# Bulk token attention and the last gradient stage hand-pipelined by groups of four heads, with the output projection as a stage of its own

## The chip, the cores and the metric

One core of one Trainium2 chip. The metric is device time in microseconds (us) of one execution; a median stands for three or more executions. The kernel computes one forward pass and all gradients of a model with two attention branches.

## The reference, cut to what matters

```python
def _B_ref(x, mem0, Wq, Wk, Wv, Wo, seg_len):      # x: 1 x 2048 x 576, 32 heads of 128, 8 memory rows, segments of 32
    mask = (idx[:, None] < M) | (idx[:, None] >= idx[None, :])
    mem = mem0
    for s in range(n_seg):                          # 64 segments, one after the other
        h = jnp.concatenate([mem, xs], axis=1)
        q, k, v = (einsum('btd,dhe->bhte', h, W) for W in (Wq, Wk, Wv))
        p = _softmax(where(mask, einsum('bhqe,bhke->bhqk', q, k) * scale, -1e9))
        o = einsum('bhte,hed->btd', einsum('bhqk,bhke->bhqe', p, v), Wo)
        mem = o[:, :M, :]                           # the memory rows go on to the next segment
        outs.append(o[:, M:, :])
    return jnp.concatenate(outs, axis=1)
g = _sigmoid((x * gate_w).sum(-1, keepdims=True))
return g * _A_ref(x, ...) + (1 - g) * _B_ref(x, ...)   # and jax.vjp of all that
```

The memory rows form a chain over the segments, which the kernel runs first. Token rows only read the finished memory, so their attention is done afterwards in bulk: 16 tiles of 128 tokens, each in 8 groups of four heads, 128 groups in all.

## The kernel before

Bulk attention, forward and backward, of one group, and the projection at the end of a tile (loads, masks and repeated lines cut):

```python
def b_bulk(self, keep, wp, sp, psum):
    for tt in range(NTT):
        ...                                          # kmT, vmT, block-diagonal k and v of the memory: 10 transfers
        for g in range(8):
            for w in ("q", "k", "v"):                # eight loads of 128 KB, on sync and GpSimd in turn
                self.dq_eng().dma_start(xT[w][:], self.xTd[w][tt][:, 4 * g:4 * g + 4, :])
                self.dq_eng().dma_start(tok[w][:], self.xtok[w][trows, gc])
            ...                                      # dO, dOT
            ...                                      # scores -> Sp; Et = exp (ScalarE); l, r (VectorE)
            nc.gpsimd.tensor_tensor(out=Pn[:], in0=Et[:], in1=r[:]..., op=ALU.mult)
            nc.sync.dma_start(self.px_dram[tt][:, 4 * g:4 * g + 4, :], Pn[:, :, 0:128])
            PT = transp(Pn, "x_PT")
            ...                                      # o = PT v -> o_g, stored; transposed into oTa (kept on chip)
            nc.gpsimd.tensor_tensor(out=prod[:], in0=dOT[:], in1=oT_g, op=ALU.mult)
            ...                                      # dP -> dS, stored; DT; dq, stored; memory rows -> dm_g
            for i, h in enumerate(hs):               # eight stores of 8 KB
                nc.sync.dma_start(self.mtok["dkx"][...], dm_g[r32, 0:128])
                nc.sync.dma_start(self.mtok["dvx"][...], dm_g[r32, 128:256])
        pb = psum.tile([P, 1024], F32, name="x_big", bufs=2)
        self.row_mm(pb, [(oTa[:, h, :], self.WoN[:, h, :]) for h in range(HB)])   # the tile's output projection
        ...                                          # output, gate gradient
```

The last gradient stage:

```python
def b_post(self, keep, sp, psum):
    mB, sB = ...                                     # one block-diagonal buffer each for q, dO, p, ds
    for tt in range(self.NTT):
        for w in ("q", "dO"):
            self.load_blockdiag(mB[w], self.mtok[w], tt)          # 2 x 4 transfers
        for i in range(4):
            for sl in range(4):
                for w, src in (("p", self.pmq_dram), ("ds", self.dsmq_dram)):
                    nc.sync.dma_start(sB[w][...], src[4 * tt + sl]...)   # 32 transfers
        for g in range(8):
            ...                                      # five loads, on sync and GpSimd in turn
            ...                                      # dk, dv, stored; three transposes; 24 products into pdx
```

The softmax here doesn't subtract the row's maximum and nothing guards it: scores larger than these inputs give would overflow.

Of the kernel before, what the change touches and what calls it, by code (L numbers as in the profile page):

```python
# [7 lines left out]
ALU = mybir.AluOpType  # L8
# [22 lines left out]
class Kern:  # L31
# [50 lines left out]
    def setup_B_dram(self, dram):  # L82
# [11 lines left out]
        self.mtok = {w: t(w + "m_dram", [NM, J]) for w in ("q", "k", "v", "o", "dO", "dq", "dk", "dv", "dkx", "dvx")}  # L94
# [8 lines left out]
        self.dsmq_dram = t("dsmq_dram", [NSEG, MEM, HB, 32])  # L103
        self.memT_dram = t("memT_dram", [P, NKT, NSEG, MEM])
# [281 lines left out]
    def b_bulk(self, keep, wp, sp, psum):  # L386
# [13 lines left out]
        self.maskX = mx  # L400
        vmB = [wp.tile([P, 8, 4, E], BF16, name=f"x_vmB{i}") for i in range(2)]
        kmB = [wp.tile([P, 8, 4, E], BF16, name=f"x_kmB{i}") for i in range(2)]
        for t in vmB + kmB:
            nc.gpsimd.memset(t[:], 0.0)
        dgacc = keep.tile([P, D], F32, name="dgacc")
        nc.vector.memset(dgacc[:], 0.0)
        for tt in range(NTT):
            trows = slice(tt * P, (tt + 1) * P)
            mT = {}
            for w in ("k", "v"):  # L410
                mT[w] = sp.tile([P, 4, HB, 8], BF16, name=f"x_{w}mT", bufs=2)
                nc.sync.dma_start(mT[w][:], self.mTd[w][4 * tt:4 * tt + 4].rearrange("s p h t -> p s h t"))
            vB, kB = vmB[tt % 2], kmB[tt % 2]
            self.load_blockdiag(vB, self.mtok["v"], tt)
            self.load_blockdiag(kB, self.mtok["k"], tt)
            xt = sp.tile([P, D], BF16, name="x_xt", bufs=2)
            nc.sync.dma_start(xt[:], self.A_x[trows, :])
            go = sp.tile([P, D], BF16, name="x_go", bufs=2)
            nc.sync.dma_start(go[:], self.grad_out[trows, :])
            at = sp.tile([P, D], BF16, name="x_at", bufs=2)  # L420
            nc.sync.dma_start(at[:], self.a_dram[trows, :])
            oTa = sp.tile([P, HB, P], BF16, name="x_oTa", bufs=1)
            for g in range(8):
                hs = range(4 * g, 4 * g + 4)
                gc = slice(512 * g, 512 * g + 512)
                xT, tok = {}, {}
                for w in ("q", "k", "v"):
                    xT[w] = sp.tile([P, 4, P], BF16, name=f"x_{w}T", bufs=3)
                    self.dq_eng().dma_start(xT[w][:], self.xTd[w][tt][:, 4 * g:4 * g + 4, :])
                    tok[w] = sp.tile([P, 512], BF16, name=f"x_{w}", bufs=3)  # L430
                    self.dq_eng().dma_start(tok[w][:], self.xtok[w][trows, gc])
                dO_g = sp.tile([P, 512], BF16, name="x_dO", bufs=3)
                self.dq_eng().dma_start(dO_g[:], self.xtok["dO"][trows, gc])
                dOT = sp.tile([P, 512], BF16, name="x_dOT", bufs=3)
                self.dq_eng().dma_start(dOT[:], self.xTd["dO"][tt][:, 4 * g:4 * g + 4, :].rearrange("p h t -> p (h t)"))
                Sp = psum.tile([P, 4, 256], F32, name="x_big", bufs=2)
                for b in range(2):
                    self.mm(Sp[:, 2 * b:2 * b + 2, 0:160], lhsT=self.identB[:], rhs=self.maskX[:], start=True, stop=False)
                for i, h in enumerate(hs):
                    q_h = xT["q"][:, i, :]  # L440
                    self.mm(Sp[:, i, 0:128], lhsT=q_h, rhs=xT["k"][:, i, :], start=False, stop=False)
                    self.mm(Sp[:, i, 128:160], lhsT=q_h, rhs=mT["k"][:, :, h, :], start=False, stop=True)
                Et = sp.tile([P, 4, 160], BF16, name="x_E", bufs=2)
                nc.scalar.activation(Et[:], Sp[:, :, 0:160], ACT.Exp, scale=SCALEB)
                l = sp.tile([P, 4], F32, name="x_l", bufs=2)
                nc.vector.tensor_reduce(out=l[:], in_=Et[:], axis=AX.X, op=ALU.add)
                r = sp.tile([P, 4], F32, name="x_r", bufs=2)
                nc.vector.reciprocal(r[:], l[:])
                Pn = sp.tile([P, 4, 160], BF16, name="x_P", bufs=3)
                nc.gpsimd.tensor_tensor(out=Pn[:], in0=Et[:], in1=r[:].unsqueeze(2).to_broadcast([P, 4, 160]), op=ALU.mult)  # L450
                nc.sync.dma_start(self.px_dram[tt][:, 4 * g:4 * g + 4, :], Pn[:, :, 0:128])

                def transp(src, nm):
                    pt = psum.tile([P, 640], BF16, name="x_tr", bufs=2)
                    for i in range(4):
                        self.tr(pt[:, 128 * i:128 * i + 128], src[:, i, 0:128], P)
                    for i in range(4):
                        self.tr(pt[32 * i:32 * i + 32, 512:640], src[:, i, 128:160], P, tp=(0, 32 * i))
                    o = sp.tile([P, 640], BF16, name=nm, bufs=2)
                    nc.vector.tensor_copy(o[:], pt[:])  # L460
                    return o

                def transp4(src, dst):
                    pt = psum.tile([P, 640], BF16, name="x_tr", bufs=2)
                    for i in range(4):
                        self.tr(pt[:, 128 * i:128 * i + 128], src[:, 128 * i:128 * i + 128], P)
                    nc.vector.tensor_copy(dst, pt[:, 0:512])

                PT = transp(Pn, "x_PT")
                po = psum.tile([P, 512], F32, name="x_po", bufs=2)  # L470
                self.mm(po[:], lhsT=PT[:, 512:640], rhs=vB[:, g].rearrange("p i e -> p (i e)"), start=True, stop=False)
                for i, h in enumerate(hs):
                    self.mm(po[:, 128 * i:128 * i + 128], lhsT=PT[:, 128 * i:128 * i + 128],
                            rhs=tok["v"][:, 128 * i:128 * i + 128], start=False, stop=True)
                o_g = sp.tile([P, 512], BF16, name="x_o", bufs=3)
                nc.scalar.copy(o_g[:], po[:])
                nc.sync.dma_start(self.xtok["o"][trows, gc], o_g[:])
                oT_g = oTa[:, 4 * g:4 * g + 4, :].rearrange("p h t -> p (h t)")
                transp4(o_g, oT_g)
                prod = sp.tile([P, 512], BF16, name="x_prod", bufs=2)  # L480
                nc.gpsimd.tensor_tensor(out=prod[:], in0=dOT[:], in1=oT_g, op=ALU.mult)
                dP = psum.tile([P, 4, 256], F32, name="x_big", bufs=2)
                for i, h in enumerate(hs):
                    hc = slice(128 * i, 128 * i + 128)
                    self.mm(dP[:, i, 0:128], lhsT=dOT[:, hc], rhs=xT["v"][:, i, :], start=(i % 2 == 0), stop=False)
                    self.mm(dP[:, i, 128:160], lhsT=dOT[:, hc], rhs=mT["v"][:, :, h, :], start=False, stop=False)
                    self.mm(dP[:, i, 0:160], lhsT=prod[:, hc], rhs=self.negones[:], start=False, stop=True)
                dS = sp.tile([P, 4, 160], BF16, name="x_dS", bufs=3)
                nc.vector.scalar_tensor_tensor(out=dS[:], in0=dP[:, :, 0:160], scalar=SCALEB, in1=Pn[:],
                                               op0=ALU.mult, op1=ALU.mult)  # L490
                nc.sync.dma_start(self.dsx_dram[tt][:, 4 * g:4 * g + 4, :], dS[:, :, 0:128])
                DT = transp(dS, "x_DT")
                pq = psum.tile([P, 512], F32, name="x_po", bufs=2)
                self.mm(pq[:], lhsT=DT[:, 512:640], rhs=kB[:, g].rearrange("p i e -> p (i e)"), start=True, stop=False)
                for i, h in enumerate(hs):
                    self.mm(pq[:, 128 * i:128 * i + 128], lhsT=DT[:, 128 * i:128 * i + 128],
                            rhs=tok["k"][:, 128 * i:128 * i + 128], start=False, stop=True)
                dq_g = sp.tile([P, 512], BF16, name="x_dq", bufs=3)
                nc.scalar.copy(dq_g[:], pq[:])  # L499
                nc.sync.dma_start(self.xtok["dq"][trows, gc], dq_g[:])  # L500
                pk = psum.tile([P, 512], F32, name="x_po", bufs=2)
                for i, h in enumerate(hs):
                    r32 = slice(32 * i, 32 * i + 32)
                    self.mm(pk[r32, 0:128], lhsT=dS[:, i, 128:160], rhs=tok["q"][:, 128 * i:128 * i + 128], tp=(0, 32 * i))
                    self.mm(pk[r32, 128:256], lhsT=Pn[:, i, 128:160], rhs=dO_g[:, 128 * i:128 * i + 128], tp=(0, 32 * i))
# [937 lines left out]
```

## Time and profile before

| what | before |
|---|---|
| median | 9572.9 us (9568.9 to 9580.3, 4 runs) |
| bulk with projection, 3720 to 5400 | 1680 us, 13.1 us a group |
| backward chain beside the other branch, 5400 to 7562 | 2162 us |
| last gradient stage, 7562 to 8602 | 1040 us |
| granted TensorE clock in bulk, in the last stage | 0.63, 0.81 |

A stage is read from a window of the trace: busy time of each engine, the granted clock, and the mean share in which the 16 DMA engines were busy. The prediction shows the windows and waits of bulk. One line more, the largest wait of TensorE in the last stage (who waited, for whom; us in total, times, longest):

```profile
PE y_pk L66 <- DMA y_dsB<-dsmq_dram: 364.1, 15, 24.7
```

### The profile page before, as it was taken

To read this page: it belongs to the slowest core of one execution; us is meant where nothing else is said; L and a number is where in the kernel's file an instruction comes from. 1 tells how busy PE (TensorE), PEld (TensorE's weight loads), DVE (VectorE), ACT (ScalarE), POOL (GpSimd) and SP (SyncE) were. 2 spreads that over 40 slices of the span, in tenths; PEclk is the share of its full clock that TensorE was granted. 3 is DMA by queue.
4 is the path that set the end of the run, shared out by engine and by line. 5 is a ranking of instruction groups with operands and counts; after the bars stand their busy time and mean duration, and the time that the engine had idled before them with its cause. 6 is when DMAs were issued, how large, how long until landed. Compare 5 with 4: busy or idle time off the path is not lost. (4 is left out here: it accounts for less than half of the span.)

```text
span 9566.9 us, 226296 instructions
## 1 busy us (share of the span) xinstructions
PE 7831.6 (82%) x91018; PEld 3772.5 (39%) x91416; DVE 4114.3 (43%) x7885; ACT 3642.1 (38%) x6854; POOL 1360.6 (14%) x2452
## 2 busy tenths in 40 slices
PE   7899899999999995555555499999999856565997
PEld 2444444444444442333333244444444333333444
DVE  4222266666666662222222277777777511111001
ACT  2333355555555552111111166666666411111000
POOL 2000000011001103333333200000000111111002
PEclk9999788888888886666666688888888688788998
DMA  3554422222222223555555533333333344446443
GB/s 110 208 198 180 169 35 37 35 36 36 37 35 36 37 34 103 144 140 142 144 141 144 162 75 74 75 74 74 76 74 75 91 118 133 116 131 240 148 149 129
DMA packets 1667936, 1002.79 MB, mean 105 GB/s; under 512 B 1103017, under 2 KB 1568498, under 8 KB 1644546
## 3 DMA queue, kind: packets, MB, share of 16 engines
q1 hardware_dynamic: 1596354, 733.66, 29.8%
q0 software_dynamic: 70528, 254.63, 8.1%
q8 instruction: 716, 11.73, 0.5%
q14 instruction: 338, 2.77, 0.1%
HBM read 597.23 MB, written 390.53 MB: 103 GB/s over the span
## 5 line engine op out<-in xcount | busy, mean ns | idle before, releaser
L1052 DVE TENSOR_TENSOR a_W<-a_dP,a_E 128x512 bf16<-128x512 f32 x2048 | 1328.3, 686 | 797.3 <-PE a_dP L66 757.3
L1185 DVE TENSOR_TENSOR b_dS<-b_dP,b_E 128x512 bf16<-128x512 f32 x2048 | 1313.6, 684 | 611.9 <-PE b_dP L66 509.1
L1018 ACT ACTIVATE a_E<-a_S 128x512 bf16<-128x512 f32 x2048 | 1137.9, 598 | 649.7 <-PE a_dP L66 550.2
L1164 ACT ACTIVATE b_E<-b_S 128x512 bf16<-128x512 f32 x2048 | 1110.0, 595 | 505.0 <-PE b_dP L66 307.8
L66 PE MATMUL b_dP<-b_KV,b_QD 32*128 32x512 bf16 x2048 | 663.9, 444 | 21.3 <-DVE b_dS L1185 20.9
L66 PE MATMUL b_S<-b_KV,b_QD 32*128 32x512 bf16 x2048 | 550.4, 446 | 116.0 <-DMA b_QD<-qd_dram 92.8
L66 PE MATMUL a_dP<-a_QD,l_KV 32*128 32x512 bf16 x2048 | 590.9, 424 | 49.9 <-DVE a_W L1052 49.9
L66 PE MATMUL a_S<-a_QD,l_KV 32*128 32x512 bf16 x2048 | 560.7, 424 | 8.7 <-DMA a_QD<-qd_dram 8.0
L66 PE MATMUL w_acc<-w_d,w_h 128*128 128x512 bf16 (+1 forms) x2352 | 522.5, 380 | 38.5 <-DMA w_d<-dqx_dram 35.8
L731 DVE COPY y_T<-y_pt 128x512 bf16<-128x512 bf16 x384 | 151.2, 422 | 888.3 <-PE y_pt L71 888.3
L66 PE MATMUL r_pj<-WT,r_dT 128*32 128x288 bf16 x12288 | 497.7, 309 | 0.0
L63 ACT CAST p_tok<-p_pb 128x512 bf16<-128x512 f32 x512 | 299.5, 586 | 514.1 <-PE p_pb L66 514.1
L66 PE MATMUL b_acc<-b_dS,b_SD 128*32 128x512 bf16 x2048 | 475.3, 460 | 0.0
L66 PE MATMUL b_acc<-b_E,b_SD 128*32 128x512 bf16 x2048 | 474.9, 460 | 0.0
L61 DVE COPY p_tT<-p_pt 128x512 bf16<-128x512 bf16 x512 | 217.5, 425 | 597.0 <-PE p_pt L71 596.8
L66 PE MATMUL a_acc<-a_E,l_VK 128*64 128x512 bf16 x2048 | 443.4, 429 | 24.3 <-DVE a_acs L1060 24.3
L66 PE MATMUL a_acc<-a_W,l_WK 128*64 128x512 bf16 x2048 | 462.5, 448 | 0.0
L66 PE MATMUL y_pdx<-WT,y_T 128*128 128x512 bf16 (+1 forms) x2977 | 422.3, 287 | 23.1 <-ACT y_dx L737 10.9
L499 ACT CAST x_dq<-x_po 128x512 bf16<-128x512 f32 x128 | 75.0, 586 | 939.2 <-PE x_po L66 879.2
L66 PEld LDWEIGHTS <-r_dT 128*32 128x32 bf16 x12288 | 350.8, 105 | 114.5 <-issue 19.9
L66 PEld LDWEIGHTS <-WoN 128*128 128x128 bf16 (+1 forms) x10080 | 338.4, 110 | 100.0 <-issue 100.0
L66 PEld LDWEIGHTS <-w_h 128*128 128x128 bf16 (+1 forms) x2400 | 237.2, 100 | 323.5 <-issue 57.9
(408 smaller groups left out, 12300.3 us busy)
## 6 DMA issues: line engine op xcount, KB each, us to landing
b_QD<-qd_dram SPq DMA_DIRECT2D x256, 128.0 KB
b_SD<-sd_dram SPq DMA_DIRECT2D x256, 128.0 KB
dOx_dram<-p_tok SPq DMA_DIRECT2D x16, 1024.0 KB
dOxT_dram<-p_tT POOLq DMA_DIRECT2D x16, 1024.0 KB, 5.5
kx_dram<-p_tok SPq DMA_DIRECT2D x16, 1024.0 KB
kxT_dram<-p_tT POOLq DMA_DIRECT2D x16, 1024.0 KB, 5.3
vx_dram<-p_tok SPq DMA_DIRECT2D x16, 1024.0 KB
vxT_dram<-p_tT POOLq DMA_DIRECT2D x16, 1024.0 KB, 5.4
```

The costliest lines, as they stand in the source:

```text
L61: nc.vector.tensor_copy(out, in_)
L63: nc.scalar.copy(out, in_)
L66: return self.nc.tensor.matmul(out, lhsT, rhs, start=start, stop=stop, tile_position=tp, skip_group_check=True)
L499: nc.scalar.copy(dq_g[:], pq[:])
L731: nc.vector.tensor_copy(tT[:], pt[:])
L1018: nc.scalar.activation(E_[m][:], S.pop(m)[:, :], ACT.Exp, scale=SCALEA)
L1052: nc.vector.tensor_tensor(out=W_[m][:], in0=dP[:], in1=E_[m][:], op=ALU.mult)
L1164: nc.scalar.activation(E_[m][:], S.pop(m)[:, :], ACT.Exp, scale=SCALEA)
L1185: nc.vector.tensor_tensor(out=D_[m][:], in0=dP[:], in1=E_[m][:], op=ALU.mult)
```

## The change

The intent: break the chain of engines within a group. Seven groups are in flight in bulk and three in the last stage, in hand order (`manual_schedule`: the instructions stay in the order in which the program writes them), each stage of a group one round later than the stage before it. Loads go out three groups ahead, all on the sync queue. The projection leaves bulk (its accumulator's place goes to the pipeline) and reads the transposed o back from DRAM. The four pieces of dm (what the memory rows get of the gradients of k and v) are stored as four transfers of 16 KB instead of eight of 8 KB. The last stage gets two sets of block-diagonal buffers.

```diff
-            for g in range(8):
-                ... one group from loads to dm, as above
+        def load(t):
+            ...
+            for w, nb in (("k", 4), ("q", 4), ("v", 8), ("dO", 8)):
+                d[w + "T"] = sp.tile([P, 4, P], BF16, name=f"x_{w}T", bufs=nb)
+                nc.sync.dma_start(d[w + "T"][:], self.xTd[w][tt][:, 4 * g:4 * g + 4, :])
+            for w, nb in (("v", 6), ("k", 10), ("q", 10), ("dO", 10)):
+                d[w] = sp.tile([P, 512], BF16, name=f"x_{w}", bufs=nb)
+                nc.sync.dma_start(d[w][:], self.xtok[w][tt * P:(tt + 1) * P, 512 * g:512 * g + 512])
+        def st_OT(t):
+            ...
+            nc.scalar.copy(oT[:], pt[:, 0:512])
+            nc.sync.dma_start(self.oxT_dram[tt][:, 4 * g:4 * g + 4, :], oT[:]...)
+        def st_Q(t):
+            ...
+            for i in range(4):
+                nc.sync.dma_start(self.dmx_dram[tt * 32:(tt + 1) * 32, :, h * E:(h + 1) * E], dm[32 * i:32 * i + 32])
+        stages = (st_S, st_T, st_O, st_OT, st_D, st_DT, st_Q)
+        with self.tc.manual_schedule():
+            for t in range(3):
+                load(t)
+            for t in range(NG + len(stages) - 1):
+                for n, st in enumerate(stages):
+                    if 0 <= t - n < NG:
+                        st(t - n)
+                load(t + 3)
+    def b_out(self, wp, sp, psum):
+        for tt in range(self.NTT):
+            nc.sync.dma_start(oTa[:], self.oxT_dram[tt])
+            ...
+            self.row_mm(pb, [(oTa[:, h, :], self.WoN[:, h, :]) for h in range(HB)])
+            ...                                      # ScalarE copy, four VectorE steps -> dz16
+            self.mm(pg[0:1, 0:512], lhsT=dz16[:, 0:1], rhs=xt[:, 0:512])     # the gate row
     def b_post(self, keep, sp, psum):
-        mB = {w: keep.tile([P, 8, 4, E], BF16, name=f"y_{w}B") for w in ("q", "dO")}
+        mB = {w: [keep.tile([P, 8, 4, E], BF16, name=f"y_{w}B{i}") for i in range(2)] for w in ("q", "dO")}
+            if g == 4 and tt + 1 < self.NTT:
+                load_tile(tt + 1)                    # the 40 transfers, on sync
+        stages = (st_KV, st_T, st_H)
```

## The prediction

> **What bounds the kernel now.** I read the page first (its slices and its list of groups), then cut the span into stages with the busy-time windows, then read the waits, the single-tile views and the timeline in the two stages that the change rewrites. The windows are:
>
> ```profile
> core 0: us, PE busy (x) PEld busy (x) DVE busy (x) ACT busy (x) POOL busy (x), PEclk, DMA share, GB/s
> ...
> 3720.00:5400.00 1680.00, 952.55 (x8624) 578.52 (x8735) 462.72 (x895) 282.43 (x528) 588.13 (x773) 0.63 0.52 139
> ...
> 7562.00:8602.00 1040.00, 638.10 (x5776) 373.94 (x5887) 151.23 (x384) 160.14 (x273) 166.72 (x314) 0.81 0.43 124
> ```
>
> The first row is the bulk attention with the output projection inside it: 1680 us for 128 groups of four heads, 13.1 us a group. No engine is above 57%. The second row is the last gradient stage: 1040 us for 128 groups. Everything outside these rows (6847 us) runs the same instructions after the change, so I carry it over unchanged.
>
> In bulk the waits of TensorE show a chain, not a full engine:
>
> ```profile
> PE x_big L66 <- POOL x_prod L481: 255.3, 128, 4.8
> PE x_po L66 <- DMA x_v<-vx_dram: 152.7, 32, 6.8
> PE x_tr L71 <- DVE x_dS L489: 101.1, 108, 1.3
> PE x_tr L71 <- POOL x_P L450: 59.2, 17, 7.3
> ```
>
> A group is scores, exp, sum, reciprocal, normalise, transpose, o, transpose o, product, dP, dS, transpose, dq. Each step waits for another engine, and at most two groups overlap. GpSimd makes P and prod and issues half the loads too. The granted clock is only 0.63.
>
> In the last stage the picture is different. Two windows of one tile (eight groups):
>
> ```profile
> 7567.00:7601.00 34.00, 32.84 (x319) 19.52 (x324) 8.27 (x21) 8.20 (x14) 9.05 (x17) 1.00 0.64 192
> 7601.00:7634.00 33.00, 7.64 (x51) 4.11 (x51) 1.18 (x3) 1.81 (x3) 1.60 (x3) 0.59 0.22 53
> ```
>
> Inside a tile TensorE is full at clock 1.00. The starts of the first matmul of each group lie 4.86 us apart, again and again. Between tiles TensorE stands still: the waits give `y_pk` behind the transfer `y_dsB` 364.1 us in 15 waits, 24.3 us each. Those are single buffers, refilled by 40 transfers after the last reader of the old tile.
>
> Third, the sync queue (SPq), which the busy shares leave out. The single-tile views give the issue time of one transfer (ns, min/median/max):
>
> ```profile
> L431 SPq DMA_DIRECT2D x_k<-kx_dram x128: 320/434/1535, 3619.6 to 5357.9; - x128
> L510 SPq DMA_DIRECT2D dkxm_dram<-x_dm x512: 302/419/1782, 3745.1 to 5391.5; - x171
> L383 SPq DMA_DIRECT2D x_kmB<-km_dram x64: 539/607/610, 3728.6 to 5293.5; - x64
> L702 SPq DMA_DIRECT2D y_pB<-pmq_dram x256: 651/651/719, 7480.7 to 8557.9; - x128
> ```
>
> Adding the durations of all its records in bulk gives 1012 us of 1680, although GpSimd issues 512 loads beside it. After the change it issues all of them. That is the number on which this prediction turns.
>
> **What the Trainium skill says.** (1) "TensorE: Matmul & The Clock Gate", Part 1, the HAM clock gate: an idle window drops the array to half clock and sustained work restores it. The trace agrees: 1.00 inside a tile, 0.59 in the window with the stall, 0.63 in bulk. (2) "Perfetto Trace Analysis", "What DMA-bound means": one way to be DMA-bound is that the issuing engine's sequencer is solid DMA slices. In bulk it is 60% full now, so not yet. (3) "DMA: Bandwidth & Descriptors", "Issuing engines are not separate DMA queues": issuing from several engines only saves the sequencer's time, which is "usually small relative to the DMA itself". Here the trace differs: a 128 KB load costs 0.43 us to issue, and 128 packets of 1 KB at a mean of 56 ns over 16 engines are 0.45 us of engine time. The two are equal, so taking GpSimd out of the issuing is not free.
>
> **The change, part by part: bulk.** Instructions per group stay almost the same, but the program order staggers seven groups, so each engine finds its input made one round earlier. The chain between engines is gone. What remains is the work of each resource in a round:
> - ScalarE: exp 0.70, o 0.59, o transposed (moved here from VectorE) about 0.59, dq 0.59, dm 0.38: 2.85 us.
> - VectorE: 0.82 + 0.18 + 2 x 0.49 + 0.82 = 2.8 us. GpSimd: 1.25 + 1.15 = 2.4 us, its four issues of 0.55 gone.
> - TensorE: from the stretches in the timeline (masks and scores 1.4, transposes 0.8 twice, o 1.0, o transposed 0.4, dP 1.1, dq 1.0, memory rows 0.4) about 7 us at the clock of now; a full clock would give some 4.5.
> - DMA engines: 11 transfers of 1 KB packets x 0.45, two (P, dS) of 512 packets of 256 B at 17.8 ns = 0.57 each, the small ones about 0.8: 6.9 us.
> - Sync queue: the order of the built kernel shows 17 transfers a round (8 loads, 5 stores of 128 KB, 4 of dm) and 10 more per tile. Successive starts are about 0.046 us further apart than the duration. 8 loads x 0.475 = 3.8; P and the four other stores 0.5 + 4 x 0.43 = 2.2; dm 4 x 0.465 = 1.9 (half as many as before, twice the bytes); per tile 8 x 0.65 + 2 x 0.5 = 6.2, over 8 groups 0.8. Sum 8.7 us.
>
> A check from the other side: 1012 us plus some 2150 gaps of 0.046 is 1111; 640 more loads and stores add about 300, 512 fewer dm stores take 248 off, the loads that move to the projection 35: 1128, or 8.8 a group. I add 0.1 for waits on landings. The largest of the five sets the round: the queue, 8.9 us x 128 = 1140, and 25 for filling and draining: **1165 us**.
>
> **Output projection.** 16 tiles, each 32 products of 512 columns (0.216 us) and 32 of 64 (about 0.06) and the gate row: 8.7 us, 139 in all. Its loads hide (three buffers). A start and tail behind the barrier add 13: **152 us**. Together 1317 against 1680: 363 saved.
>
> **Last stage.** TensorE stays at 4.86 a group, 38.9 a tile. The tile's 40 transfers (8 x 0.63 + 32 x 0.695 = 27.3 us of issuing) now go into second buffers four groups ahead, but on the same in-order queue, ahead of the loads of the group three ahead. Until those land it takes 27.3 + 1.9 + 2.5 = 31.7 us. TensorE then has in hand the rest of one round (3.9) and three whole ones (14.6): 18.5. It therefore still stands for 13 us a tile in place of 24, and restarts at the low clock (about 2). A tile: 38.9 + 13 + 2 = 54; the queue's own sum, 8 x 3.1 + 27.3 = 52, agrees. 15 x 54 + 39 + 8 = **857 us**, 183 saved.
>
> Total: 9575 - 363 - 183 = 9029; I say **9030 us**.
>
> **The rivals.** (A) TensorE bounds bulk, not the queue: seven groups in flight leave it no gaps, and 7 us a round give 896 (4.5 with a full clock gives less). For it: it has the next largest sum. Against it: 8.7 of issuing is counted from measured durations. It would make about 8,770. (B) Landings bound it. The trace's records show that each sync-queue transfer signals one of eight semaphores in turn and first waits for the earlier one on it, so eight are in flight. From issue to the last arrival I find medians of 2.0 to 4.3 us. If all 18.25 took 4.3, the round would be 18.25 x 4.3 / 8 = 9.8 us, and the total about 9,145. With DMA engines busy 6.9 of 8.9 this is the likelier miss. (C) The new order buys nothing in bulk: stores that wait for compute stand ahead of the loads on one queue, and the groups end up in lockstep at 12 us; then only the last stage gains: about 9,430. Against it: loads go out three rounds ahead, and buffers (4 to 10) cover seven stages. (D) The last stage's burst is hidden wholly: 16 x 39 + 10 = 634, total 8,805. Against it: the queue needs 52 us a tile whatever TensorE does.
>
> **Range and chances.** Issuing at 0.40 to 0.52 us a transfer, or landings as in (B), moves bulk by -120 to +130; the tile stall (8 to 16 us) moves the last stage by 70. Together: 8,890 to 9,210 eight times in ten. Slower than 9,384 (no 2% gain) needs (C). Faster 0.94, same 0.05, slower 0.01.
>
> **What would show it.** In the changed profile bulk should take about 1165 us with the sync queue over 90% filled, TensorE's longest waits on loads (the transposed q and k) instead of on GpSimd's prod, and a clock under 1. The projection should be near 150 us with TensorE full. The last stage should keep 4.86 us a group, with 15 gaps of 11 to 15 us, behind a load that the burst delays. Wrong would be: a sync queue with long idle stretches in bulk (then A or C), its issues no longer but waits on its own landings (B), no gaps between tiles (D), or a change in the other 6847 us.

## The result, and the profile after

The kernel after took 9428.0 us (median; 9426.3 to 9435.9, 4 runs) beside 9572.9 before: a ratio of 0.985 (95% interval 0.983 to 0.987). That is 1.5% faster, where 9030 (5.7%) was predicted. A ratio here is the mean time of one kernel's runs over that of the other's of the same rounds, so not quite the ratio of the medians. Effects of experiments below are differences of such ratios from 0.985, times 9575 us, except where a run edits the kernel before; the stage times are read from the traces.

The windows of the kernel after, bulk, projection and last stage (busy us and instruction count of each engine, then clock, DMA share, GB/s):

```profile
core 0: us, PE busy (x) PEld busy (x) DVE busy (x) ACT busy (x) POOL busy (x), PEclk, DMA share, GB/s
3722.00:5141.00 1419.00, 746.92 (x7680) 532.43 (x7679) 333.16 (x641) 336.66 (x640) 318.95 (x265) 0.65 0.67 172
5141.00:5370.00 229.00, 158.15 (x1056) 73.17 (x1056) 53.52 (x128) 10.22 (x16) 7.07 (x15) 0.86 0.46 148
7501.00:8461.00 960.00, 634.60 (x5891) 390.35 (x5888) 152.62 (x384) 147.65 (x273) 0.00 (x0) 0.84 0.51 136
```

| part | before | after | saved | predicted |
|---|---|---|---|---|
| bulk, projection | 1680 | 1419 + 229 = 1648 | 32 | 363 |
| backward chain | 2162 | 2131 | 31 | 0 |
| last gradient stage | 1040 | 960 | 80 | 183 |
| all else | 4685 | 4686 | -1 | 0 |

(Spans of the profiled runs, 9566.9 and 9425.5 us.) In bulk and projection GpSimd lost 262 us of busy time, VectorE 76 and TensorE 47, and yet the two together hardly moved. The waits of bulk show the chain gone and a load in its place:

```profile
ACT x_o L445 <- DMA ox_dram<-x_o: 528.3, 118, 6.4
PE x_S L66 <- DMA x_qT<-qxT_dram: 472.5, 128, 12.5
PE x_po L66 <- ACT x_o L445: 189.6, 123, 3.6
```

TensorE waits once in every round for the transposed q, which it did not before; its wait for GpSimd's product fell from 255.3 to 2.6 us. ScalarE waits for stores of o. Both are transfers of the sync queue. One round of that queue, from its timeline (start, us, instruction; "x4" is four issues):

```profile
4351.49 0.53 SPq L422 DMA_DIRECT2D x_kT<-kxT_dram  x1
4352.12 0.38 SPq L422 DMA_DIRECT2D x_qT<-qxT_dram  x1
...
4354.96 0.38 SPq L425 DMA_DIRECT2D x_dO<-dOx_dram  x1
4355.43 0.38 SPq L465 DMA_DIRECT2D px_dram<-x_P  x1
4355.91 0.45 SPq L474 DMA_DIRECT2D ox_dram<-x_o  x1
4356.45 0.39 SPq L484 DMA_DIRECT2D oxT_dram<-x_oT  x1
4356.94 0.42 SPq L500 DMA_DIRECT2D dsx_dram<-x_dS  x1
4357.81 0.32 SPq L509 DMA_DIRECT2D dqx_dram<-x_o  x1
4358.65 2.52 SPq L520 DMA_DIRECT2D dmx_dram<-x_dm  x4
4361.27 0.53 SPq L422 DMA_DIRECT2D x_kT<-kxT_dram  x1
```

From one load of k to the next it is 9.8 us, with no hole over 0.6 us; the four small stores of dm take a quarter of it. A round that opens a tile has ten transfers more. Adding up the queue's records in the steady part of bulk (before 3800 to 5350 us, 119 groups of 13.0; after 3800 to 5100 us, 118 rounds of 11.0), durations with their share of the gaps of 0.04 us between records:

| in a round | before: us | after: us | predicted |
|---|---|---|---|
| loads on the sync queue (4 before, 8 after) | 1.9 | 3.7 | 3.8 |
| stores of 128 KB (4, then 5) | 1.7 | 2.4 | 2.2 |
| stores of dm (8, then 4) | 3.9 | 2.6 | 1.9 |
| transfers of a tile, over 8 groups | 1.0 | 0.75 | 0.8 |
| semaphore instructions (7.0, then 11.7) | 0.5 | 0.7 | not counted |
| waiting | 4.0 | 0.9 | 0.1 |
| sum | 13.0 | 11.0 | 8.8, taken as 8.9 |

Before, the queue had 4.0 us of room in a group of 13.0. Now it stands still for 0.9 in 11.0, and nearly all of that (97 of 106 us in these 118 rounds) is no room either, but waits for its own landings: a store waits for the transfer issued eight before it, which for the first store of dm is the load of k and for dq the load of v. The queue's own waits from 3800 to 5100 us:

```profile
SPq L520 <- DMA x_k<-kx_dram: 44.6, 76, 1.5
SPq L509 <- DMA x_v<-vx_dram: 38.0, 68, 1.5
SPq L474 <- ACT x_E L458: 33.9, 81, 0.6
```

The last of these lines is no pause of the queue: between the record before and those issues of L474 the trace leaves only some 3 us in all, so what the view counts as waiting lies within the issues themselves.

In the projection stage the largest waits of TensorE in each tile are for VectorE's last steps of the same tile:

```profile
PEld L66 <- DVE o_dz L564: 57.6, 16, 3.7
PE o_big L66 <- DVE o_tmpg L561: 34.8, 10, 3.6
PE o_big L66 <- DVE o_dz L564: 20.9, 6, 3.5
PE o_big L66 <- DMA o_xt<-in_A_x_dram: 19.2, 1, 19.2
```

The first line (weight loads) and the two after it (products) show the same 16 waits, one a tile, some 3.5 us each.

And in the last stage, against the line shown of before:

```profile
ACT y_tdk L769 <- DMA dkx_dram<-y_tdk: 305.4, 13, 25.1
PE y_pk L66 <- DMA y_q<-qx_dram: 290.2, 17, 22.4
```

There are still some 15 long waits, now behind the ordinary load of q and the ordinary store of dk, which stand behind the 40 tile transfers in the same queue. Starts of groups (the first product of ds and q) are 4.94 us apart at the median (4.86 before). The 15 longest intervals average 24.2 us (33.2 before), the others 5.19 (4.77 before).

### The profile page after: what moved, and what is told of

It reads as the page before. It is cut to its first block, busy times and chain, and to the rows that moved or that the text cites. A ratio compares the mean times of both kernels' runs of the same rounds, so it can differ in the third digit from the quotient of the medians.

```text
span 9425.5 us, 225987 instructions
## 1 busy us (share of the span) xinstructions
PE 7805.7 (83%) x91416; PEld 3821.5 (41%) x91416; DVE 4039.0 (43%) x7757; ACT 3693.6 (39%) x6982; POOL 924.2 (10%) x1624
## 4 chain that ended last, share of the span: by engine, by line
PE 60%; DMA 14%; SPq 12%; issue 7%; DVE 5%; ACT 3%; POOL 1%; ACTq 0%; DVEq 0%; POOLq 0%
PE r_pj L66 7%; PE a_acc L66 6%; PE p_pb L66 6%; PE w_acc L66 6%; PE c_pj L66 5%; PE c_x L66 4%; PE a_S L66 4%; PE b_S L66 4%; DMA ox_dram<-x_o 4%; SPq L740 3%; PE b_acc L66 3%; PE y_pdx L66 2%; PE b_dP L66 2%; DMA x_qT<-qxT_dram 2%; DMA x_k<-kx_dram 2%
## 5 line engine op out<-in xcount | busy, mean ns | idle before, releaser
L66 PE MATMUL r_pj<-WT,r_dT 128*32 128x288 bf16 x12288 | 500.7, 310 | 26.4 <-DMA WT<-st_WT 26.4
L460 DVE TENSOR_REDUCE x_l<-x_E 128x4 f32<-128x640 bf16 x128 | 104.9, 820 | 961.3 <-ACT x_E L458 937.6
L66 PE MATMUL x_S<-x_kT,x_qT 128*128 128x128 bf16 x512 | 86.7, 270 | 472.5 <-DMA x_qT<-qxT_dram 472.5
```

What stands on the lines that cost most here:

```text
L66: return self.nc.tensor.matmul(out, lhsT, rhs, start=start, stop=stop, tile_position=tp, skip_group_check=True)
L460: nc.vector.tensor_reduce(out=l[:], in_=Et[:], axis=AX.X, op=ALU.add)
```

## The experiments

Theory Q: the sync queue's issuing sets the round in bulk and the tile in the last stage. Rivals: the DMA engines' work (D), ScalarE's buffers (X), the burst of 40 as such (B, last stage). All runs gave the reference's results. Unless said otherwise the edit is to the kernel after.

### Bulk: one store of dm

```diff
-            for i in range(4):
-                h = 4 * g + i
-                nc.sync.dma_start(self.dmx_dram[tt * 32:(tt + 1) * 32, :, h * E:(h + 1) * E], dm[32 * i:32 * i + 32])
+            nc.sync.dma_start(self.dmx_dram[tt, 4 * g:4 * g + 4].rearrange("i r a e -> (i r) a e"), dm[:])
```

(the array in DRAM has its axes in this order, and its reader follows)

> The changed kernel with dm of a group stored by one transfer of 64 KB, not four of 16 KB; bytes and packets alike, three issues a round fewer. In the changed profile the four cost about 0.62 us of the sync queue each. If the sync queue's issuing sets the bulk round (theory Q): 1.8 to 1.9 us a round less, bulk 1409 -> about 1170 to 1180 us, the whole 9428 -> about 9190. If the DMA engines' work sets it (rival D): bytes are unchanged, 0 to 30 us. If ScalarE's waits for buffers of o and dq set it (rival X): little, since those stores stay, under 50 us.

Measured: 9214.7 us, ratio 0.962: 223 us taken off. From the first score product to the first product of the projection 1211 us, after 1433. The line of the stores, after and here (count: min/median/max ns):

```profile
L520 SPq DMA_DIRECT2D dmx_dram<-x_dm x512: 549/586/1511, 3794.3 to 5148.7; - x171
```

```profile
L518 SPq DMA_DIRECT2D dmx_dram<-x_dm x128: 319/320/1489, 3785.4 to 4915.6; - x128
```

One issue of 64 KB costs less than one of 16 KB did. The same bytes in three issues fewer gave nearly what Q had said, and D is out as the bound of the kernel after. The packets were not alike, against what the expectation says: 256 of 256 bytes a group became 128 of 512, which spares the DMA engines 0.07 us a group, too little to matter. But the DMA share rose to 0.81 here, so D may be next.

### Bulk: loads shared with GpSimd again

```diff
-                nc.sync.dma_start(d[w + "T"][:], ...)
+                self.dq_eng().dma_start(d[w + "T"][:], ...)      # and the same for d[w]: sync and GpSimd in turn
```

> The changed kernel with the bulk loads issued alternately by the sync queue and by GpSimd, as the kernel before did. Q: four issues a round, 1.8 us, leave the sync queue, and eight more landings may be under way: round 11.0 -> 8 to 9 us, bulk 1409 -> 1050 to 1150, the whole about 9070 to 9170. D (DMA engines bound, 0.67 busy): round cannot fall below 11 x 0.67 = 7.4 us and little should move, under 80 us. X: under 50 us.

Measured: 9190.8 us, ratio 0.960: 241 us off; first score to projection 1192 us. This undoes one part of the change, and it alone turns 1.5% into 4%. A round of the sync queue is 9.1 us, a little above what Q expected (the whole is 21 us above its range) and far from what D allows. The DMA share is 0.77; what holds the round at 9.1 was not tested. The run also lets more landings be under way, so it does not tell issues from waits on landings; the next one, which adds issues, does.

### Bulk: four more issues, same bytes

```diff
-                nc.sync.dma_start(d[w][:], ...[..., 512 * g:512 * g + 512])
+                for hf in range(2):
+                    nc.sync.dma_start(d[w][:, 256 * hf:256 * hf + 256], ...[..., 512 * g + 256 * hf:512 * g + 256 * hf + 256])
```

> The changed kernel with each of the four token-row loads in two halves: four issues of 64 KB more a round, the same bytes, packets of 512 bytes instead of 1 KB (about 0.1 us of DMA engine time a transfer more). Q: four issues of 0.46 us, 1.8 to 2.0 us a round, bulk +230 to +260 us, the whole about 9670. D: +0.3 to 0.4 us a round, +40 to +50 us. X: about 0.

Measured: 9618.6 us, ratio 1.004: 182 us more, first score to projection 1620. That is four times what D allows and three quarters of what Q expected: the round is 12.5 us, 1.5 more. The queue's records and their gaps grew by 2.0 us a round, as Q has it, and its waits shrank from 0.9 to 0.3 and took up some of that. The kernel is now 0.4% slower than before (interval 0.2 to 0.6%).

### Bulk: more buffers

```diff
-            o = sp.tile([P, 512], BF16, name="x_o", bufs=4)
+            o = sp.tile([P, 512], BF16, name="x_o", bufs=8)
```

(also x_oT 4 for 2, x_dm 6 for 3)

> The changed kernel with x_o 8 buffers for 4, x_oT 4 for 2, x_dm 6 for 3; nothing else. ScalarE waits 511 us in bulk for stores from x_o. X (these buffers stop the pipeline): bulk falls by more than 150 us. Q: that wait is the pipeline's slack showing on an engine that is not the bound; it shrinks or moves elsewhere and bulk changes by less than 40 us.

Measured: 9445.7 us, ratio 0.986, no gain. ScalarE's wait for stores of o, 528 us after, is no longer among the longest; TensorE's wait for the transposed q grew by 217 us:

```profile
PE x_S L66 <- DMA x_qT<-qxT_dram: 689.5, 128, 12.5
```

X falls. The largest wait in a list was the slack of an engine that is not the bound.

### Bulk: two loads of 512 KB for eight of 128 KB

```diff
+            nc.sync.dma_start(t4[:]..., self.xTd4[:, tt, :, 4 * g:4 * g + 4, :]...)       # kT, qT, vT, dOT in one
+            nc.sync.dma_start(k4[:], self.xtok4[:, tt * P:(tt + 1) * P, 512 * g:512 * g + 512]...)   # v, k, q, dO in one
```

> The changed kernel with the eight loads of a round merged into two of 512 KB, same bytes and packets. Q: six issues of 0.45 us fewer, 2.7 us a round less, unless the issue time grows with the number of packets (four times as many each, which then shows as about 1.8 us an issue): bulk -300 to -340, or about -50 if it grows. D: about 0.

Measured: 9426.0 us, ratio 0.984: 13 us, nothing. Six issues fewer and no gain contradicts Q as I had put it. One round of the queue:

```profile
4350.74 1.10 SPq L424 DMA_DIRECT2D x_T<-xT_dram  x1
4351.94 0.45 SPq L427 DMA_DIRECT2D x_k<-x_dram  x1
4352.48 0.46 SPq L471 DMA_DIRECT2D px_dram<-x_P  x1
4353.06 1.89 SPq L480 DMA_DIRECT2D ox_dram<-x_o  x1
4355.06 1.09 SPq L490 DMA_DIRECT2D oxT_dram<-x_oT  x1
```

The loads themselves issue in about 0.5 us at the median, with four times the bytes. It is the stores behind them that grew: o from a median of 0.455 to 1.93 us, transposed o from 0.39 to 1.09. The stores' sum in a round went from 2.2 to 4.5 us, while the loads' fell from 3.4 to 1.2. The Trainium skill's "Perfetto Trace Analysis", section "DMA Instruction — HWDGE (DVE, Sync)", says that the recorded window of such an issue holds the wait for the descriptor generator and the generating, and that the DMA engines begin earlier when the descriptors outgrow their buffer. Stores that grow behind 1 MB of loads agree with a queue that is full; no record shows that buffer itself. Two runs test whether the burst is to blame.

### Bulk: loads for two groups at a time

```diff
+            if g % 2 == 0:
+                pr[w + "T"] = sp.tile([P, 8, P], BF16, name=f"x_{w}T", bufs=nb)
+                nc.sync.dma_start(pr[w + "T"][:], self.xTd[w][tt][:, 4 * g:4 * g + 8, :])       # 256 KB, 2 KB a packet
+                ...                                                                             # and pr[w]
```

> The changed kernel with one thing: the eight loads made for two groups at a time, 256 KB in 128 packets of 2 KB, so four issues a round fewer and half the load packets. If a round is paid by the number of issues (Q): -1.8 us a round, -200 to -240 us, about 9,190 to 9,230. If merging never helps, as the run with two loads of 512 KB seemed to say: under 40.

Measured: 9240.0 us, ratio 0.964: 199 us off. Fewer issues help here. By itself this run does not rule out the packets: half as many for the loads also spare the DMA engines some time (866 us of packet time, as a mean of the 16 engines, in bulk; 957 after). The next run keeps the packets.

### Bulk: the two merged loads apart

```diff
+                    if n == 4 and t:
+                        load2(t + 2)          # the second 512 KB goes out in the middle of the round
```

> The two merged loads of 512 KB again, which gained nothing when they stood together, since the issues behind them took 1.9 and 1.1 us instead of 0.46 and 0.39. Now the second goes out in the middle of the round. If the long issues were 1 MB of backlog in front of the stores, which drains while nothing else is issued: half of it can drain during other issues, the two long issues shrink, and the whole falls by 60 to 200 us. If each 512 KB load costs the sync queue its 1.3 to 1.5 us wherever it stands: within 40 us of 9,428.

Measured: 9280.0 us, ratio 0.968: 164 us off, with the same transfers as the run that gained nothing. The store of o is back to a median of 0.33 us; the store of dq, now behind the second load, has 1.14, as it would if half of the backlog drained beside other issues. The DMA engines' time did not fall (1044 us), so that is not what was gained. The burst ate the gain, then, though not all of it is back: six issues fewer should give 300 to 340 us by Q.

### Last stage: the 40 transfers on GpSimd

```diff
-                        nc.sync.dma_start(sB[w][tt % 2][...], ...)
+                        nc.gpsimd.dma_start(sB[w][tt % 2][...], ...)       # and the eight of load_blockdiag
```

> The changed kernel with the 40 transfers per tile of the last gradient stage issued by GpSimd, which has little to do there. If the stall of some 20 to 24 us a tile is the sync queue's sum (60 us of issuing a tile, theory Q): the queue is left with about 34 us a tile, below TensorE's 39.5, and the stage falls from 960 to 640 to 700 us, the whole 9428 -> about 9110 to 9170. If the stall is the DMA engines' time for the small packets of the burst (rival D): the stage stays above 880.

Measured: 9106.5 us, ratio 0.950: 331 us off. The stage's window:

```profile
7514.00:8143.00 629.00, 587.47 (x5793) 362.96 (x5793) 148.78 (x378) 145.25 (x270) 313.35 (x560) 0.99 0.76 206
```

TensorE is busy 587 of 629 us at a clock of 0.99, and no interval between the starts of groups is over 5.1 us (4.94 at the median). D falls: the same bytes arrive in time. Their packet records differ (61,440 of 64 and 256 bytes on the sync queue, some 9,000 of 32 to 4096 bytes on GpSimd's), but hardly the DMA engines' time for them, 54 us over the stage after and 52 here.

### Last stage: the transfers spread over six rounds, same queue

```diff
+                if nxt is not None and t % 8 < 6:
+                    for _ in range(7):
+                        next(nxt, None)                  # seven of the tile's 40 transfers
```

> The changed kernel with the 40 transfers per tile spread over six rounds, seven a round, on the same sync queue. If the stall comes from the burst standing ahead of the loads (rival B): it goes, stage 960 -> about 650 to 700. If the queue's sum a tile sets it (Q): the sum stays at 58 to 60 us a tile, and the stage falls only from 960 to 880 to 950.

Measured: 9407.8 us, ratio 0.982: 33 us off; the stage is 921 us. The burst is gone, and so are the intervals of 24 us (the 28 longest average 10.4), but groups now start 7.2 us apart at the median. B falls, Q stands: the queue's own sum in a tile is 56.7 us (51.1 of records, 5.6 of gaps) of 58.9 (mean of the 14 tiles from the second burst on).

### Last stage: on GpSimd, single buffers

```diff
-                self.load_blockdiag(mB[w][tt % 2], self.mtok[w], tt, nc.gpsimd)
+                self.load_blockdiag(mB[w][0], self.mtok[w], tt, nc.gpsimd)     # after the last reader of the old tile
```

> The last stage with its 40 transfers on GpSimd but into single buffers again, after the last reader of the old tile: the hand order and GpSimd kept, the double buffer undone. If the double buffer is what lets the stall go, once the queue has room: 40 issues of 0.56 us and a landing of 2.5 come back per tile, 15 x 20 to 25 us: stage 629 -> 930 to 1010, the whole about 9,400 to 9,480. If GpSimd's queue alone had been the cure: under 9,200.

Measured: 9467.0 us, ratio 0.987; the stage takes 978 us, and the stall of before is back:

```profile
PE y_pk L66 <- DMA y_dsB<-dsmq_dram: 321.9, 15, 23.4
```

So second buffers and room in the queue are both needed. Against before, hand order with second buffers gave 80 us, hand order with GpSimd 62, all three together 411. The two without the hand order were not run.

### Projection: the gate row one tile late

```diff
+                self.row_mm(pb, [(oTa[:, h, :], self.WoN[:, h, :]) for h in range(HB)])
+                if late:
+                    gate(*late)              # the gate row of the tile before; loads two tiles ahead
```

> The changed kernel with the projection stage in hand order: the gate row's product of a tile after the big product of the next, loads two tiles ahead. If the 13.1 us a tile is TensorE waiting for the chain projection, ScalarE copy, four VectorE steps, gate row: a tile falls to 8.7 to 9.5 us, the stage 239 -> 155 to 170, the whole -70 to -85. If it is the loads (1.4 MB in three buffers): under 20 us.

Measured: 9360.1 us, ratio 0.977: 77 us off. From the first product to the last gate row it is 142.7 us instead of 213.9, 8.9 a tile instead of 13.4. The run moves the loads as well, but the waits shown above name VectorE in every tile and a load once.

### Projection: inside bulk again

```diff
-            nc.sync.dma_start(self.oxT_dram[tt][:, 4 * g:4 * g + 4, :], oT[:]...)
+            oT = oTa[tt][:, 512 * g:512 * g + 512]          # stays on chip
+            pb = psum.tile([P, 4, 256], F32, name="x_S", bufs=1)...   # one product per tile, between two score products
```

> The changed kernel with one part undone: the projection inside the bulk as before. The transposed o stays on chip (one store of 128 KB a round fewer), a tile's product runs in the buffer of the scores, the gate row one round later. If the projection cost 239 us because it stands alone (TensorE idle beside it in bulk): -240 for the stage, -55 for the stores gone, +30 for its own transfers, +50 to +100 for 16 products of 9 us that hold up the round: the whole -165 to -215, about 9,215 to 9,265. If it is work that TensorE has no room for: under 60.

Measured: 9170.6 us, ratio 0.958: 262 us off, more than I allowed. Bulk with the projection in it takes 1390 us, less than the 1419 without: one store of 128 KB has left the queue in each round, and TensorE does the products in time in which it had stood idle (its busy time rose by 80 us, its clock from 0.65 to 0.72). Two more changes nearly cancel: the last stage, whose code is the same, takes 914 us for 960, for a reason that was not looked for, and the backward chain 2165 for 2131, as before the change.

### The kernel before, with one store of dm

```diff
-                for i, h in enumerate(hs):
-                    nc.sync.dma_start(self.mtok["dkx"][...], dm_g[r32, 0:128])
-                    nc.sync.dma_start(self.mtok["dvx"][...], dm_g[r32, 128:256])
+                nc.sync.dma_start(self.dmx_dram[tt, 4 * g:4 * g + 4]..., dm_g[:])
```

> The kernel before with dm stored in one transfer a group instead of eight: seven issues, about 3.2 us of a 13.1 us group, leave the sync queue. If the kernel before was bound by the chain of engines in each group (what the prediction read) and its queue had room: within 30 us of before, 9,550 to 9,610. If its queue was the bound already and the hand order itself gave nothing: -200 to -400, and then the new order deserves no credit for what the other runs gain.

Measured: 9438.0 us, ratio 0.985: 140 us off the kernel before (medians of the same rounds), between the two expectations. A third of the 3.2 us that left the queue came off the group (13.0 to 12.0 us). So the queue was part of the chain of before too, though it had 4 us of room; which of its waits that was I did not separate. Bulk with projection is 1542 us here. The changed kernel with the same store needs 1211 for bulk alone and 214 for the projection after it: 117 us less than 1542 is what the rest of the change is worth here.

### What helped, together

The edits shown above for one store of dm, loads by pairs of groups, the 40 transfers on GpSimd and the late gate row, in one kernel:

> Everything that helped, with the loads on one queue: dm in one transfer, loads of two groups at a time (256 KB in packets of 2 KB: four issues a round for eight, and still 128 packets each), the last stage's 40 transfers on GpSimd, the gate row late. Q: sync queue about 6 us a round, under the DMA engines' 6.8 to 7.2 (estimated from 0.81 of 9.4 us with dm in one, less for the longer packets): bulk 900 to 1000 us, last stage 630, projection 165; the whole 8,530 to 8,650. If the DMA engines set the bulk round already at 9.4 us (dm in one): bulk stays near 1150 and the whole near 8,800.

Measured: 8590.3 us, ratio 0.897, in the range of Q. From first score to projection 987 us. The queue's records and gaps are 6.8 us of a round of 7.6, though, not 6, and the DMA share is 0.86: which of the two binds now is open.

Then the same with the projection inside bulk in place of the late gate row, one pair buffer fewer for five of the loads, and

```diff
-                    self.load_blockdiag(mB[w][tt % 2], self.mtok[w], tt)
+                    self.load_blockdiag(mB[w][tt % 2], self.mtok[w], tt, nc.gpsimd)     # in bulk too
```

> The two before it together: dm in one, loads by pairs of groups, the tile transfers of bulk and of the last stage on GpSimd, the projection inside the bulk. Sync queue about 4.7 us a round, DMA engines about 6.5, TensorE (742 + 142 us of busy time) 6.9 at the clock of the changed kernel: bulk with projection 900 to 1010 us in place of 1409 + 239, last stage 630: the whole 8,350 to 8,550. If something else in the hand order holds the round near 9 us: about 8,700.

Measured: 8425.3 us, ratio 0.879 (0.878 to 0.880): 12% faster than before, the best kernel here. Its windows of bulk with projection and of the last stage:

```profile
3743.00:4662.00 919.00, 671.91 (x8643) 466.75 (x8735) 392.87 (x785) 345.31 (x656) 388.39 (x389) 0.89 0.87 253
6828.00:7457.00 629.00, 583.03 (x5691) 363.88 (x5800) 148.88 (x379) 146.09 (x272) 313.07 (x560) 0.99 0.74 206
```

A round is 7.1 us. The DMA engines are 0.87 busy, TensorE 0.73 at a clock of 0.89, and the sync queue's records and gaps fill 6.0 of the 7.1 us. Which of them a next step should relieve was not tested.

## Why the prediction was right or wrong

**Right: what would bind.** The prediction named the sync queue as the bound of bulk, TensorE's wait for the transposed q as its sign, and a clock under 1. All three are in the trace (the queue's records and gaps fill 10.1 of 11.0 us a round, over the 90% that it gave as a sign), and the runs that add and remove issues confirm the first.

**Wrong by size: "The largest of the five sets the round: the queue, 8.9 us x 128 = 1140."** The queue sets it at 11.0 us. The loads were right (3.7 for 3.8). Three terms were not. The dm stores were put at "4 x 0.465 = 1.9", the cost of the old 8 KB ones; the new ones take 0.586 at the median and 2.6 in a round. The 11.7 semaphore instructions cost 0.7 us in a round and were left out, though records of them stood in the trace of before. Waits were put at 0.1 and are 0.9. With 0.2 for the five stores that makes the 2.2 us between the sums of the table, 2.1 above the 8.9 that was used: 128 x 2.1 = 269 us; bulk missed by 254 (1419 for 1165). The check "from the other side" could not find it, since it took the old cost for the new stores too, and counted 2150 gaps where the trace of before has 3153 records.

**Wrong rival, near its number.** Rival C (lockstep behind stores) gave 9,430, which is what was measured, but not for its reason: the queue hardly pauses for computing engines (at most 9 of the 106 us in which it stood still), and the saving of the last stage was not 183 either. That number is luck. Rival B (landings) has a part in the miss: nearly all of the 0.9 us of waits, where 0.1 was allowed. The issues are the larger part.

**Projection: "8.7 us a tile", "Its loads hide".** The loads did hide, but in the program's order the gate row of a tile stood before the next tile's product, behind a copy and four VectorE steps: 13.4 us a tile. One tile later it is 8.9, near the 8.7, but in part by luck: the terms of that sum add to 8.8 before the gate row, and a product of 64 columns takes 0.029 us from start to start in the trace of before, half of the 0.06 assumed. And the sum of the stage, 229 against 152, does not tell its price: the product had been nearly free in bulk, as the run with it inside shows.

**Last stage: "stands for 13 us a tile in place of 24".** It stands for 19.3 (24.2 less a group) in place of 28.3 by the same measure, and the other intervals grew from 4.77 to 5.19. The text worked the stall from the burst alone and used the queue's sum, 52 us a tile, as a check that agreed with 54. The sum is what binds, and the run with the transfers spread shows it at 56.7 without its waits: a load or store costs 0.47 us with its gap for 0.44 (56 in a tile), the semaphore instructions, missing here too, some 2 us. With waits it is 60.6 us a tile in the kernel after, 960 in all for 857.

**Not foreseen: 31 us in the backward chain.** At its start TensorE stands still for 65.4 us before (27.4 for a transfer of weights, 25.8 for one into b_QD, 12.2 for GpSimd) and for 26.4 after. This goes with the projection as a stage: from the chain's first product to the last stage the four kernels without that stage take 2148 to 2155 us, the thirteen with it 2118 to 2139. How it does so was not tested. "Everything outside these rows" did not quite stay.

## What to carry to other kernels

Before moving loads from one issuing queue to another, add up that queue's records for one round, with the durations of the very shapes that it will issue, its semaphore instructions and its waits: here the pipeline broke the chain between engines, and then the issuing queue was the next engine in line. Fewer and wider transfers helped as long as no burst of them stood ahead of a store that the pipeline needed; work that left a stage with idle TensorE time was no longer free. And the second buffers paid only once the transfers that fill them had a queue with room.

## What the Trainium skill lacked or had wrong

- "DMA: Bandwidth & Descriptors", "Issuing engines are not separate DMA queues", says that issuing from several engines saves only the sequencer's time, "usually small relative to the DMA itself". Here that time was the bound: moving half of the loads to GpSimd took 241 us off, moving the last stage's 40 transfers a tile took 331 us off, the bytes unchanged and the DMA engines' own time nearly so (957 to 915 us in bulk, 487 to 478 in the last stage).
- The same page, "Rules for kernel authors", advises coalescing small transfers and 1 MiB or more per DMA, and does not say what a wide transfer does to the issues behind it. Merging eight loads of 128 KB into two of 512 KB gained 13 us, no more than noise, since the issue of a store behind them grew from 0.455 to 1.93 us; the same two loads apart gained 164 us, and 256 KB in packets of 2 KB gained 199 us.
- None of the pages read gives what an issue costs by shape. Here, at the median: 0.38 us for most loads of 128 KB on the sync queue, 0.586 for a store of 16 KB from 32 partitions, 0.320 for one of 64 KB from 128 partitions, 0.651 for a piece of the block-diagonal p (0.561 on GpSimd).
- None gives the cost of semaphore instructions on an issuing queue. Here 11.7 of them took 0.7 us of an 11.0 us round.
